# Decode attention with a gated feed-forward: keys transposed four sets ahead of their scores, the first four sets loaded between the gate's pieces

## The chip, the core and the metric

One core of a Trainium2 chip runs the whole program. The time is the device time of one execution in microseconds; of the kernel before there are three such runs. One further execution was recorded by the hardware profiler, and its trace is what the profile is made of.

## What is computed

Eight sequences, one new token each. The token is normalised, asks a window of 1024 cached keys per key-value head, and the attention's output is multiplied by a gate that a feed-forward network computes from the same normalised token:

```python
xn = _layernorm(x)                              # x: 8 x 1 x 512, bf16
q = (xn @ wq).reshape(B, 1, 32, 128)            # 32 query heads
k = k_cache[:, :, Sk - W:, :]                   # 8 x 8 heads, last W = 1024 of 4096 keys, 128 wide
v = v_cache[:, :, Sk - W:, :]                   # each key-value head serves 4 query heads
p = softmax((q . k) * 128 ** -0.5)
s = (p . v).reshape(B, 1, 4096) @ wo
g = silu((gelu(xn @ w_gate) * (xn @ w_up)) @ w_down)   # hidden width 1792
out = x + s * g
```

## The kernel before

A *group* is one pair of sequence and key-value head: 1024 keys by 128 numbers. There are 64 groups. A *set* is four groups (QG = NB = 4), so there are 16 sets (NQ), and one set of keys or of values is one load of 1 MB.

**Loads.** All large loads stand in the queue of SyncE (SP) in the order of lines 164 to 177: four pieces of the gate and up weights (`load_up`, 0.9 MB each), two of the down weights (`load_down`), four of Wq (`load_q`, 1 MB), the keys of sets 0 and 1, and then, for each set q, the keys of set q + 2, the values of set q, and after every second set 0.5 MB of Wo. They add up to 47.46 MB. All but Wo go through one ring of 16 buffers of 1 MB (`ring`, NRING, line 75): the seventeenth load waits until everything that reads the first has run.

**Front.** While the first weights come, TensorE runs constant products (`keep_busy`, line 233: a 128 x 128 matrix of ones by 512 columns of ones, into a PSUM tile that nobody reads). Then come the transposes of the normalised token, the products of the four pieces of gate and up (`ffn_up`, L274), GELU on VectorE and ScalarE (`ffn_act`, three steps, L288 to L307), the down products (`ffn_down`, L313), SiLU (`ffn_gate`), and the query products (L349), copied to `qT_all` (L358). After each of these pieces stands a `keep_busy`.

**Loop.** Lines 512 to 535 write out the order of the work by hand; each engine runs its own instructions in that order. In pass q, for each of the four groups i:

- `transposes` of the next group: eight 128 x 128 products of keys with the identity into one of two PSUM buffers (L368), then a copy of five eighths by VectorE (kTa, L375) and of three eighths by ScalarE (kTb, L377) into one of three buffers of `kT_pool`;
- `scores` (L397) of this group: transposed keys as weights, 16 columns of queries. A set's four groups share one PSUM bank; a mask product (L386) opens it;
- `values` (L476) of the set q - 2 (LAG = 2), with their `sums` (L451) before the first group;
- in group 1 `max_all` of the set before (L416 to L426), in group 2 `exponentials` of it: a second mask product (L437) adds the maximum, and ScalarE takes the exponential (L446).

At the end of a pass stand `normalise` of the finished set (L487) and `max_keys` (L408) of the set just scored. Two sets later the output projection of a key-value head (`project`, L502) is mixed in. After the last pass the last four heads are projected, multiplied by the gate, transposed, added to x and written out (lines 538 to 547).

The order of the front, in the kernel's own lines:

```python
    for n in range(NDC):
        ffn_up(n)
        keep_busy(5)
    for step in range(3):
        ffn_act(step)
    keep_busy(4)
    for d in range(NDC):
        ffn_down(d)
        keep_busy(2)
```

Of the kernel before, what the change touches and what calls it, by code (L numbers as in the profile page):

```python
# [11 lines left out]
BF16 = mybir.dt.bfloat16  # L12
# [5 lines left out]
def kernel(  # L18
# [33 lines left out]
    nc = tc.nc  # L52
# [3 lines left out]
    Hkv, Sk, Dh = A_k_cache.shape[1], A_k_cache.shape[2], A_k_cache.shape[3]  # L56
    Hq = A_wq.shape[1] // Dh
    rep = Hq // Hkv
    W = min(4096, max(256, Sk // 4))
    win0 = Sk - W  # L60
    F = B_w_gate.shape[1]
    P = nc.NUM_PARTITIONS
    NDC = D // P
    NFC = F // P
    NSC = W // P
# [5 lines left out]
    NB = QG  # L71
    NCS = QG * NSC
    VC = 4
    AC = 3
    NRING = 16
    MASK = -1.0e30
    NG = Hkv * B
    NQ = NG // QG
    QC = QG * rep
    SH = B // QG  # L80
    LAG = 2
# [3 lines left out]
    persist = ctx.enter_context(tc.tile_pool(name="persist", bufs=1))  # L85
    ffn_sb = ctx.enter_context(tc.tile_pool(name="ffn_sb", bufs=1))
    ring = ctx.enter_context(tc.tile_pool(name="ring", bufs=NRING))
    kT_pool = ctx.enter_context(tc.tile_pool(name="kT_pool", bufs=3))
    p_pool = ctx.enter_context(tc.tile_pool(name="p_pool", bufs=4))
    small = ctx.enter_context(tc.tile_pool(name="small", bufs=2))  # L90
    ps_misc = ctx.enter_context(tc.tile_pool(name="ps_misc", bufs=1, space=PSUM))
    ps_kT = ctx.enter_context(tc.tile_pool(name="ps_kT", bufs=2, space=PSUM))
# [16 lines left out]
    q_sb, up_sb, dn_sb, k_sb, v_sb = {}, {}, {}, {}, {}  # L109

    def buffer(n):
        return ring.tile([P, NL], BF16, name="ring_sb")[:, 0:n]

    def load_set(cache, q):
        hkv, b = divmod(q * QG, B)
        t = buffer(NL)
        nc.sync.dma_start(
            out=t,
            in_=cache[b : b + QG, hkv, win0:Sk, :].rearrange(
                "g (e c) d -> e g (c d)", c=NCS  # L120
            ),
        )
        return t

    def load_k(q):
        k_sb[q] = load_set(A_k_cache, q)

    def load_v(q):
        v_sb[q] = load_set(A_v_cache, q)

    def load_q(k):
        q_sb[k] = buffer(Hq * Dh)
        nc.sync.dma_start(out=q_sb[k], in_=A_wq.rearrange("(p k) n -> p k n", k=NDC)[:, k, :])

    def load_up(n):

        w = (B_w_gate, B_w_up)[n % 2]
        k = n // 2 * UPK
        up_sb[n] = buffer(UPK * F).rearrange("p (k n) -> p k n", k=UPK)
        nc.sync.dma_start(  # L140
            out=up_sb[n],
            in_=w.rearrange("(p k) n -> p k n", k=NDC)[:, k : k + UPK, :],
        )

    def load_down(n):
        dn_sb[n] = buffer(DNJ * D).rearrange("p (j d) -> p j d", j=DNJ)
        nc.sync.dma_start(
            out=dn_sb[n],
            in_=B_w_down.rearrange("(p j) d -> p j d", j=NFC)[
                :, n * DNJ : (n + 1) * DNJ, :  # L150
            ],
        )

    def load_wo(hkv):
        nc.sync.dma_start(
            out=wo_sb[:, hkv * rep : (hkv + 1) * rep, :],
            in_=A_wo[hkv * rep * Dh : (hkv + 1) * rep * Dh, :].rearrange(
                "(k p) d -> p k d", p=P
            ),
        )  # L160
# [2 lines left out]
    nc.scalar.dma_start(out=x_sb, in_=A_x.flatten_outer_dims())  # L163
    for n in range(NDC):
        load_up(n)
    for n in range(2):
        load_down(n)
    for k in range(NDC):
        load_q(k)
    for q in range(LAG):  # L170
        load_k(q)
    for q in range(NQ):
        if q + LAG < NQ:
            load_k(q + LAG)
        load_v(q)
        if q % SH == SH - 1:
            load_wo(q // SH)
# [4 lines left out]
    ident = consts.tile([P, P], BF16, name="ident")  # L182
    nc.vector.memset(ident, 0.0)
    nc.gpsimd.affine_select(
        out=ident,
        in_=ident,
# [14 lines left out]
        out=row_of,  # L201
        in_=row_of,
# [9 lines left out]
        out=other,  # L212
        in_=other,
# [19 lines left out]
    def keep_busy(n):  # L233
        for _ in range(n):
            nc.tensor.matmul(idle_ps, ones_w[:, 0:P], ones_w, start=True, stop=True)  # L235

    keep_busy(8)


    stats = persist.tile([B, nc.vector.BN_STATS_DIM], FP32, name="stats")  # L240
# [5 lines left out]
        out=rstd, in_=mv[:, 1:2], func=ACT.Sqrt, bias=eps_sb, scale=1.0  # L246
# [4 lines left out]
        out=xhat,  # L251
# [7 lines left out]
    for k in range(NDC):  # L259
        nc.tensor.transpose(  # L260
            xnT_ps[:, k, :], xhat[:, k::NDC], ident[0:B, 0:B]
        )
    nc.vector.tensor_copy(out=xnT_sb, in_=xnT_ps)


    ffn = {}

    def ffn_up(n):
        if n == 0:
            ffn["gu"] = ps_misc.tile([P, NFC, 2, B], FP32, name="gu_ps", tag="misc")  # L270
        for j in range(NFC):
            for i in range(UPK):
                k = n // 2 * UPK + i
                nc.tensor.matmul(  # L274
                    ffn["gu"][:, j, n % 2, :],
                    up_sb[n][:, i, j::NFC],
                    xnT_sb[:, k, :],
                    start=(n == 0 and j == 0 and i == 0),
                    stop=(k == NDC - 1),
                    skip_group_check=True,  # L280
                )

    def ffn_act(step):
        zT = ffn["gu"][:, :, 0, :]
        uT = ffn["gu"][:, :, 1, :]
        if step == 0:
            z2 = ffn["z2"] = ffn_sb.tile([P, NFC, B], FP32, name="z2")
            nc.scalar.activation(out=z2, in_=zT, func=ACT.Square)  # L288
        elif step == 1:
            z2 = ffn["z2"]  # L290
            nc.vector.tensor_scalar(  # L291
                out=z2, in0=z2, scalar1=0.044715, scalar2=1.0, op0=ALU.mult, op1=ALU.add
            )
            u3 = ffn_sb.tile([P, NFC, B], FP32, name="u3")
            nc.vector.tensor_tensor(out=u3, in0=z2, in1=zT, op=ALU.mult)
            th = ffn["th"] = ffn_sb.tile([P, NFC, B], FP32, name="th")
            nc.scalar.activation(
                out=th, in_=u3, func=ACT.Tanh, scale=0.7978845608028654
            )
        else:  # L300
            gm = ffn_sb.tile([P, NFC, B], FP32, name="gm")
            nc.vector.tensor_scalar(
                out=gm, in0=ffn["th"], scalar1=0.5, scalar2=0.5, op0=ALU.mult, op1=ALU.add
            )
            gz = ffn_sb.tile([P, NFC, B], FP32, name="gz")
            nc.vector.tensor_tensor(out=gz, in0=gm, in1=zT, op=ALU.mult)
            nc.vector.tensor_tensor(out=hT_sb, in0=gz, in1=uT, op=ALU.mult)  # L307
# [24 lines left out]

    for n in range(NDC):
        ffn_up(n)
        keep_busy(5)
    for step in range(3):
        ffn_act(step)
    keep_busy(4)
    for d in range(NDC):
        ffn_down(d)  # L340
        keep_busy(2)
    for step in range(2):
        ffn_gate(step)

# [2 lines left out]
    for k in range(NDC):  # L347
        for m in range(Hq):
            nc.tensor.matmul(  # L349
                qT_ps[:, m, :],  # L350
                q_sb[k][:, m * Dh : (m + 1) * Dh],
                xnT_sb[:, k, :],
                start=(k == 0 and m == 0),
                stop=(k == NDC - 1),
                skip_group_check=True,
            )
        keep_busy(5 if k < NDC - 1 else 3)
    nc.vector.tensor_copy(out=qT_all, in_=qT_ps.rearrange("p h b -> p b h"))  # L358


    kT, sc, pT, mxs, shift, recip = {}, {}, {}, {}, {}, {}

    def transposes(g):
        q, i = divmod(g, NB)
        kT_ps = ps_kT.tile([P, W], BF16, name="kT_ps")
        for c in range(NSC):
            n = i * NSC + c
            nc.tensor.transpose(  # L368
                kT_ps[:, c * P : (c + 1) * P],
                k_sb[q][:, n * Dh : (n + 1) * Dh],  # L370
                ident,
            )
        own = (NSC - AC) * P
        ta = kT_pool.tile([P, own], BF16, name="kTa")
        nc.vector.tensor_copy(out=ta, in_=kT_ps[:, 0:own])  # L375
        tb = kT_pool.tile([P, W - own], BF16, name="kTb")
        nc.scalar.copy(out=tb, in_=kT_ps[:, own:])  # L377
        kT[g] = [ta[:, c * P : (c + 1) * P] for c in range(NSC - AC)]
        kT[g] += [tb[:, c * P : (c + 1) * P] for c in range(AC)]

    def scores(g):
        q, i = divmod(g, NB)
# [126 lines left out]
            )  # L509


    transposes(0)
    for q in range(NQ + LAG):
        v = q - LAG
        for i in range(NB):
            g = q * NB + i
            if g + 1 < NG:
                transposes(g + 1)
            if i == 1 and 1 <= q <= NQ:
                max_all(q - 1)  # L520
            if g < NG:
                scores(g)
            if v >= 0:
                if i == 0:
                    sums(v)
                values(v * NB + i)
            if i == 2 and 1 <= q <= NQ:
                exponentials(q - 1)
            if v >= SH and v % SH == 0 and i >= NB // 2:
                for h in range(2):  # L530
                    project((v // SH - 1) * rep + (i - NB // 2) * 2 + h)
        if v >= 0:
            normalise(v)
        if q < NQ:
            max_keys(q)
# [42 lines left out]
```

## Time and profile before

| | us |
|---|---|
| median of three runs (lowest, highest) | 127.41 (127.36, 128.65) |
| the profiled execution | 127.63 |
| its span, first to last instruction | 125.8 |
| first gate piece landed, its first product | 5.82 |
| loop: first transposes | 33.45 |
| last load issued by SP | 104.79 |
| output's DMA issued | 123.42 |

The span is what the trace covers; the execution's time holds some 1.8 us around it. In the profile PE is TensorE, DVE VectorE, ACT ScalarE, SP SyncE; "L368" is line 368 of the kernel. A line of the chain of waits gives a start, a length, the engine, the tile written, the line and the number of instructions merged. The chain is followed back from the last instruction, at each step to what released it. A matmul's own duration holds its passage through the array, so durations of a run of matmuls overlap; how fast they go is read from the length of a run divided by their number. A line of the windows gives the busy time of PE, its weight load, DVE, ACT and POOL with the number of instructions, then the granted TensorE clock, the busy share of the DMA engines and GB/s.

### The profile page before, as it was taken

Reading aid. Unit: us, or ns where it says so; the run is one execution under the profiler, and the core shown is the slowest. Engines: PE = TensorE matmul, PEld = TensorE weight load, DVE = VectorE, ACT = ScalarE, POOL = GpSimd, SP = SyncE. Lnnn points to the kernel's source line nnn. Section 1 sums busy time; section 2 is a strip of 40 time slices with the busy share of each in tenths; the row PEclk is TensorE's granted clock in tenths of the full one; section 3 lists DMA queues with packets and bytes.
Section 4 is the critical chain, followed back from the end, with each engine's and each line's share of the span. In section 5 each row is a group of like instructions: output and inputs, shape, how many; then the busy total and the mean of one; then the engine's idle time right before and its main releaser. Section 6 shows DMA issues by size and latency. Waiting matters only on the chain.

```text
span 125.8 us, 4887 instructions
## 1 busy us (share of the span) xinstructions
PE 114.7 (91%) x2197; PEld 89.6 (71%) x2202; DVE 64.5 (51%) x200; ACT 42.5 (34%) x86; POOL 1.2 (1%) x7
## 2 busy tenths in 40 slices
PE   5899999989989999999999898989999999988780
PEld 1366663657777788887888787878787877877570
DVE  5200003010248768756786664858667677765531
ACT  4000005000054644543534254354544435352210
POOL 3000000000000000000000000000000000000000
PEclk9999999999999999999999999999999999999999
DMA  4999999999999999999999999999999999998300
GB/s 89 410 431 417 429 412 417 419 432 427 417 414 398 427 417 417 402 421 435 412 398 431 419 401 424 412 417 412 413 435 410 411 432 411 407 411 357 135 5 3
DMA packets 10325, 47.78 MB, mean 380 GB/s; under 512 B 816, under 2 KB 4928, under 8 KB 5696
## 3 DMA queue, kind: packets, MB, share of 16 engines
q1 hardware_dynamic: 10288, 47.46, 92.5%
q8 instruction: 17, 0.28, 0.9%
q14 instruction: 4, 0.03, 0.1%
q10 hardware_dynamic: 16, 0.01, 0.0%
HBM read 47.46 MB, written 0.01 MB: 377 GB/s over the span
## 4 chain that ended last, share of the span: by engine, by line
PE 73%; DVE 9%; ACT 6%; issue 5%; DMA 4%; ACTq 0%; DVEq 0%
PE kT_ps L368 19%; PE idle_ps L235 12%; PE o_ps L476 10%; PE sc_ps L397 9%; DVE kTa L375 6%; ACT kTb L377 6%; PE gu_ps L274 5%; DMA ring_sb<-in_B_w_gate_dram 4%; PE sc_ps L437 4%; PE sc_ps L386 4%; PE sT_ps L502 3%; PE sums_ps L451 3%; PE qT_ps L349 3%; PE fT_ps L313 1%; DVE mx L408 0%
## 5 line engine op out<-in xcount | busy, mean ns | idle before, releaser
L377 ACT COPY kTb<-kT_ps 128x384 bf16<-128x384 bf16 x64 | 30.6, 479 | 52.6 <-DVE kTa L375 52.6
L375 DVE COPY kTa<-kT_ps 128x640 bf16<-128x640 bf16 x64 | 31.3, 489 | 20.7 <-PE kT_ps L368 20.3
L368 PE MATMUL kT_ps<-ident,ring_sb 128*128 128x128 bf16 x512 | 39.1, 219 | 0.2 <-issue 0.2
L368 PEld LDWEIGHTS <-ring_sb 128*128 128x128 bf16 x512 | 29.4, 97 | 2.4 <-issue 2.2
L476 PE MATMUL o_ps<-pT,ring_sb 128*128 128x64 bf16 (+1 forms) x512 | 25.2, 190 | 2.2 <-issue 2.2
L235 PE MATMUL idle_ps<-ones_w 128*128 128x512 bf16 x53 | 20.0, 521 | 2.2 <-DVE ones_w L181 1.5
L476 PEld LDWEIGHTS <-ring_sb 128*128 128x128 bf16 x512 | 19.1, 97 | 3.0 <-issue 2.8
L397 PE MATMUL sc_ps<-qT_all,kTa 128*128 128x16 bf16 x320 | 17.8, 171 | 0.0
L397 PEld LDWEIGHTS <-kTa 128*128 128x128 bf16 x320 | 14.7, 96 | 4.2 <-issue 2.3
L397 PE MATMUL sc_ps<-qT_all,kTb 128*128 128x16 bf16 x192 | 14.5, 171 | 1.6 <-ACT kTb L377 0.4
L235 PEld LDWEIGHTS <-ones_w 128*128 128x128 bf16 x58 | 6.0, 121 | 8.8 <-issue 6.1
L397 PEld LDWEIGHTS <-kTb 128*128 128x128 bf16 x192 | 9.3, 96 | 3.3 <-ACT kTb L377 1.0
L408 DVE TENSOR_REDUCE mx<-sc_ps 128x16 f32<-128x512 f32 x16 | 10.9, 681 | 0.0
L446 ACT ACTIVATE pT<-sc_ps 128x512 bf16<-128x512 f32 x16 | 9.6, 601 | 2.7 <-PE sc_ps L437 2.6
L274 PEld LDWEIGHTS <-ring_sb 128*128 128x128 bf16 x112 | 7.4, 162 | 2.2 <-issue 1.6
L274 PE MATMUL gu_ps<-xnT_sb,ring_sb 128*128 128x8 bf16 x112 | 7.3, 201 | 0.5 <-DMA ring_sb<-in_B_w_gate_dram 0.5
L291 DVE TENSOR_SCALAR z<-z 128x112 f32<-128x112 f32 x1 | 0.2, 219 | 13.7 <-ACT z L288 13.7
L437 PE MATMUL sc_ps<-diag,ones_pp 48*128 48x512 bf16 x16 | 6.2, 386 | 0.4 <-DVE diag L426 0.4
L451 PE MATMUL sums_ps<-pT,ones_pp 128*128 128x64 bf16 x128 | 6.3, 192 | 0.0
L386 PE MATMUL sc_ps<-other,row_of 4*128 4x512 bf16 x16 | 6.2, 385 | 0.0
L502 PEld LDWEIGHTS <-wo_sb 128*128 128x128 bf16 x128 | 4.3, 96 | 2.5 <-issue 2.5
L502 PE MATMUL sT_ps<-oT_all,wo_sb 128*128 128x8 bf16 x128 | 5.4, 167 | 0.3 <-DVE oT_all L487 0.3
(54 smaller groups left out, 59.4 us busy)
## 6 DMA issues: line engine op xcount, KB each, us to landing
ring_sb<-in_A_k_cache_dram SPq DMA_DIRECT2D x16, 1024.0 KB, 18.8
ring_sb<-in_A_v_cache_dram SPq DMA_DIRECT2D x16, 1024.0 KB, 18.6
ring_sb<-in_A_wq_dram SPq DMA_DIRECT2D x4, 1024.0 KB, 19.5
wo_sb<-in_A_wo_dram SPq DMA_DIRECT2D x8, 512.0 KB, 17.8
ring_sb<-in_B_w_gate_dram SPq DMA_DIRECT2D x2, 896.0 KB, 5.0
ring_sb<-in_B_w_up_dram SPq DMA_DIRECT2D x2, 896.0 KB, 8.4
ring_sb<-in_B_w_down_dram SPq DMA_DIRECT2D x2, 896.0 KB, 12.9
x_sb<-in_A_x_dram ACTq DMA_DIRECT2D x1, 8.0 KB
```

Source lines behind the costliest of these rows:

```text
L235: nc.tensor.matmul(idle_ps, ones_w[:, 0:P], ones_w, start=True, stop=True)
L274: nc.tensor.matmul(ffn["gu"][:, j, n % 2, :], up_sb[n][:, i, j::NFC], xnT_sb[:, k, :], start=(n == 0 and j == 0 and i == 0), stop=(k == ND ...
L368: nc.tensor.transpose(kT_ps[:, c * P : (c + 1) * P], k_sb[q][:, n * Dh : (n + 1) * Dh], ident,)
L375: nc.vector.tensor_copy(out=ta, in_=kT_ps[:, 0:own])
L377: nc.scalar.copy(out=tb, in_=kT_ps[:, own:])
L386: nc.tensor.matmul(sc[q], row_of.rearrange("g e s -> g (e s)"), other.rearrange("g s j -> g (s j)") .unsqueeze(1) .to_broadcast([QG, NCS, ...
L397: nc.tensor.matmul(sc[q][:, i * NSC + c, :], kT[g][c], qT_all[:, b : b + QG, hkv * rep : (hkv + 1) * rep], start=False, stop=False, skip_g ...
L408: nc.vector.tensor_reduce(out=mx, in_=sc[q].rearrange("p c n -> p n c"), axis=AX.X, op=ALU.max)
L437: nc.tensor.matmul(sc[q], ones_pp[0 : LO + QC, :], shift[q].unsqueeze(1).to_broadcast([LO + QC, NCS, QC]), start=False, stop=True, skip_gr ...
L451: nc.tensor.matmul(sums_ps, ones_pp, pT[q][:, c * NB : (c + 1) * NB, :], start=(c == 0), stop=(c == NSC - 1),)
L476: nc.tensor.matmul(o_ps[q][:, 0:wide, :], v_sb[q][:, n * Dh : (n + 1) * Dh], pT[q][:, n : n + wide, :], start=(n == 0), stop=(n == NCS - 1 ...
L502: nc.tensor.matmul(sT_ps[0][:, d, :], wo_sb[:, h, d * P : (d + 1) * P], oT_all[:, h, :], start=(h == 0 and d == 0), stop=(h == Hq - 1), sk ...
```

## The change

The transposes run four sets ahead of the scores (LEAD = 4) instead of one group. The keys of the first four sets are loaded alternately with the four gate pieces, and each set is transposed after the piece before it; all `keep_busy` after the first, which has six products instead of eight, are taken out. Further keys are loaded four sets earlier than before, counted against the values. `kT_pool` grows from 3 to 19 buffers, the ring shrinks from 16 to 12. The GELU steps stand before the transposes of set 3. `transposes` itself is unchanged and only moves up in the file.

```diff
-    NRING = 16
+    NRING = 12
+    LEAD = 4
-    kT_pool = ctx.enter_context(tc.tile_pool(name="kT_pool", bufs=3))
+    kT_pool = ctx.enter_context(tc.tile_pool(name="kT_pool", bufs=LEAD * NB + 3))
     for n in range(NDC):
         load_up(n)
+        load_k(n)
...
-    for q in range(LAG):
+    for q in range(LEAD, LEAD + LAG):
         load_k(q)
     for q in range(NQ):
-        if q + LAG < NQ:
-            load_k(q + LAG)
+        if q + LEAD + LAG < NQ:
+            load_k(q + LEAD + LAG)
         load_v(q)
...
-    keep_busy(8)
+    keep_busy(6)
...
     for n in range(NDC):
         ffn_up(n)
-        keep_busy(5)
-    for step in range(3):
-        ffn_act(step)
-    keep_busy(4)
+        if n == NDC - 1:
+            for step in range(3):
+                ffn_act(step)
+        for i in range(NB):
+            transposes(n * NB + i)
     for d in range(NDC):
         ffn_down(d)
-        keep_busy(2)
...
-        keep_busy(5 if k < NDC - 1 else 3)
...
-    transposes(0)
     for q in range(NQ + LAG):
         v = q - LAG
         for i in range(NB):
             g = q * NB + i
-            if g + 1 < NG:
-                transposes(g + 1)
+            if g + LEAD * NB < NG:
+                transposes(g + LEAD * NB)
```

## The prediction

> **What bounds it now.** I read the page first (busy shares, slices, chain shares), then the chain of waits in order of time, then the windows of the last microseconds.
>
> ```profile
> span 125.8 us, 4887 instructions
> PE 114.7 (91%) x2197; PEld 89.6 (71%) x2202; DVE 64.5 (51%) x200; ACT 42.5 (34%) x86; POOL 1.2 (1%) x7
> PE 73%; DVE 9%; ACT 6%; issue 5%; DMA 4%; ACTq 0%; DVEq 0%
> q1 hardware_dynamic: 10288, 47.46, 92.5%
> ```
>
> Two resources are nearly full: TensorE (91%) and the 16 DMA engines (92.5%). The chain is TensorE's, with data waited for only at its head (4%). The chain in order of time shows how fast TensorE goes:
>
> ```profile
> 15.20 2.15 PE idle_ps L235 x5
> 17.35 1.61 PE gu_ps L274 x28
> 19.20 3.62 PE idle_ps L235 x8
> 22.82 0.35 PE fT_ps L313 x14
> ...
> 29.18 1.10 PE idle_ps L235 x5
> 30.28 0.78 PE qT_ps L349 x32
> ...
> 33.61 0.46 PE kT_ps L368 x8
> 34.09 0.50 DVE kTa L375
> 34.62 0.49 ACT kTb L377
> 35.38 0.48 PE kT_ps L368 x8
> ...
> 42.56 0.32 PE sc_ps L386
> ...
> 111.92 0.32 PE sc_ps L386
> ...
> 120.51 0.92 PE o_ps L476 x32
> ```
>
> A 512-column product takes 0.43 us up to 22.6 us (2.15/5) and 0.22 afterwards (1.10/5); a narrow one 57 ns (1.61/28), then 25 (0.35/14). So TensorE ran at half rate for 22.6 us, although the granted-clock column says 1.00 there. What raised it stands before the switch: eight constant products back to back, 19.20 to 22.6. The same eight from 1.52 on (to 4.93 at 0.43 each) did not, nor did 13 us of 2.15 us constant products alternating with 1.61 us of narrow ones.
>
> The mask product L386 opens each set: from 42.56 to 111.92 are 13 sets, 5.33 us each. Adding the parts of a set (transposes 4 x 0.46, scores 4 x 0.29, values 4 x 0.25, sums 0.25, two masks 0.64, maximum 0.11, projection 0.29) gives 5.28: TensorE is packed, and its waits for the two copies (DVE 9% and ACT 6% of the chain) lie beside scores and values and cost it some 0.05 us a set. The values end at 121.43; 4.4 us of projection, output and its DMA end the span.
>
> ```profile
> 115.00:116.00 1.00, 0.95 (x21) 0.65 (x18) 0.88 (x3) 0.29 (x1) 0.00 (x0) 1.00 0.81 318
> 118.00:119.00 1.00, 0.64 (x17) 0.60 (x16) 0.93 (x4) 0.00 (x0) 0.00 (x0) 1.00 0.30 105
> 119.00:120.00 1.00, 0.94 (x25) 0.64 (x25) 0.03 (x2) 0.53 (x1) 0.00 (x0) 1.00 0.00 0
> 125.60:125.70 0.10, 0.00 (x0) 0.00 (x0) 0.00 (x0) 0.00 (x0) 0.00 (x0) 0.50 0.00 0
> ```
>
> The last two columns are DMA share and GB/s, before them the clock. The input stream ends at 119.0, only 2.4 us ahead of the last values. The last line is the clock falling to half after the last product (122.96): the 3.4 us before it hold four 128-column and a few 8-column products, some 0.2 us of columns, 6%.
>
> **The profiled run** took 127.63, 1.83 more than its span; the median of the three runs is 127.41. I sum against 127.63 and take off 0.2.
>
> **The change, part by part.**
>
> *The stream.* Bytes are the same, so its end stays at 119.0. At the page's 417 GB/s, anchored on the first piece (0.92 MB, landed at 5.8), a load lands at 3.6 us + MB/0.417. In the new order: K set 0 (1.97 MB) 8.3; the gate's pieces 1 to 3 at 10.5, 15.2, 20.0 with K 1 to 3 between and after, K 3 at 22.5; down 26.9; last piece of Wq (13.9 MB) 36.9, where the old order (9.7 MB) gave 26.9; K 4 39.4; V 0 (18.1 MB) 47.0 instead of about 37; then one V every 5.67 us (2.36 MB a set) to V 9 at 97.3; V 15 between 116.1 and 117.7.
>
> *Ring of 12 instead of 16.* A load waits for the readers of the load 12 earlier. V 1 waits for set 3's transposes (at the latest 31 by the sum below) and the stream reaches it at 49.5; K 15 waits for K 9's transposes in pass 5 (about 75) and is reached at 92. SP's queue holds these waits, and behind them only further loads stand, with 18 us in hand. Cost nothing; if TensorE were 18 us later, the stream would wait too.
>
> *Constant products.* 52 go: 24 after the gate pieces at 0.43 = 10.2 us of TensorE, 26 in the down and query products at 0.22 = 5.6, and 2 at the start, in front of x-hat. None carries data. Their time is filled by transposes or by waits for data; their other effect, the clock, is priced below.
>
> *Sixteen transpose groups moved to the front.* Passes 12 to 15 lose 16 x 0.46 = 7.4 us of TensorE, 1.84 each. Their 32 copies move too: at the front DVE and ACT are idle but for the GELU steps, which stand in their queues before the copies of set 3. That chain took 2.7 us (19.0 to 21.7); two groups fill the two PSUM buffers, the other two wait for it, and so do the down products behind them.
>
> *Copies no longer waited for by scores*: 0.05 x 12 passes, 0.6 us at most, by the packing above. I put nothing.
>
> *Front at half rate.* A transpose is 128 columns, so a quarter of 0.43: 0.107 us, 0.85 a group. With two buffers a group takes (0.85 + 0.49 + 0.48 + about 0.25 of hand-overs)/2 = 1.04; a set 4.15 (at full rate 1.77 for two groups, 3.55). Gate piece 0 runs 5.8 to 7.5, set 0 8.3 to 12.4, then 1.65 + 4.15 alternately: piece 3 ends at 25.4, GELU at 28.2, set 3 at 31.0; down 56 x 57 ns = 3.2, 34.2; gate 0.8, 35.0; four query blocks of 1.84, 42.3. At full rate the pieces wait for data instead (3.55 + 0.8 is under the 4.73 us of a pair's bytes), queries end at about 38, and pass 0 starts when K 4 lands, 39.4. In the old kernel it started at 34.4.
>
> *Which rate?* Transposes at half rate cover 0.85 of 1.04 us with columns, 82%. The trace has a stretch of 62 to 65% that did not raise the clock (2.15 us of constant products per 3.77) and one of 100% that did; 82% lies midway. The down and query products cover 4% of their time (32 x 8 columns per 2.5 us of bytes), for 8 us: next to the 6% after which the clock fell. So pass 0 starts at half rate almost surely; whether the front did I put at two to one for half rate, since the eight products of 1.52 to 4.93 also failed.
>
> The Trainium skill, "TensorE: Matmul & The Clock Gate", Part 4, speaks against the change: by it, transposes don't count as busy and full rate doesn't engage for them. No row of the old kernel can show it, for there transposes always ran among other products. Taken at its word, the clock would stay down and the sum would be that of the third rival. Part 1 there would have one busy window of some 3.4 us suffice, which the first eight products here contradict.
>
> *Pass 0 and on.* Half-rate pass 0: mask 0.43 + 4 x (0.85 + 8 x 57 ns) = 5.7 us against 3.84 in the old trace (34.44 to 38.28), columns 73 to 80%. A half-rate later pass is 3.41 + 3.68 + 0.46 + 0.86 + 0.2 + 0.46 = 9.1, so 3.7 more. For the time until the clock is back the bounds are one eight-product stretch (3.4 us) and never; I take the first pass, by the 3.4 us row.
>
> *Sum.* Pass 0 from 42.3 to 48.0; pass 1 4.2 (old 38.28 to 42.49), 52.2; passes 2 to 11 10 x 5.33, 105.5; passes 12 to 15 at 3.6, 119.9 (5.33 - 1.84 = 3.49 is the packing; the step from maximum through masks to the exponential, which transposes covered, may add up to 0.3); pass 16 2.8 and pass 17 1.3 as in the old trace, 124.0. That is 2.6 later than 121.43: 130.2 for the profiled run, 130.0 by the median.
>
> **The rivals.**
> 1. *Faster: the clock is up from the front on and holds through the query products.* Pass 0 at 39.4, pass 2 at 47.4, pass 11 at 96.0 with V 9 landing just then, 101.4; 4 x 3.6, 2.8 and 1.3: 119.9, so 1.5 less, 125.9. If passes 12 to 15 kept up with the stream (3.15 us for 1.31 MB), the values would end 0.9 after V 15, 118.9: 124.9, the floor. It decides if the products at 31 to 39 us run at 25 ns. For it: transposes are half of a set's columns in the old loop, and the clock held there. Against: the 6% row.
> 2. *Front up, pass 0 down*: 39.4 + 5.7 + 4.2 + 53.3 + 14.4 + 4.1 = 121.1, 0.3 less: 127.1, no difference.
> 3. *Slower by much: the loop doesn't raise the clock soon.* Each further half-rate pass adds 3.7: two more give 137; all of them 42.3 + 5.7 + 6.6 + 10 x 9.1 + 4 x 5.7 + 5.8 = 174, a time of about 180. For it: 73 to 80% lies below the 100% that was needed. Against: masks and sums lift some 3.4 us stretches to 88%.
> 4. *The change doesn't free the loop*: with V ten us later in the stream, TensorE waits for values in the middle passes. At full rate pass 11 may start at 96.0 by data and at 95.4 by work, so this costs 0.6, and is in rival 1.
>
> **How the numbers follow.** About 1% (126.1 to 128.7) is what can be told from no change. Rival 1 gets 0.25, rival 2 0.15, the forecast and its neighbours (a front or one more pass at half rate, 128.7 to 134) 0.38, rival 3 beyond 134 0.22. The range runs from the floor, 125.0, to two further half-rate passes, 137; what is left out is some 0.04 below and 0.14 above. The forecast's own range is 128 to 133.
>
> **What would show it.** Right: the query products at 57 ns; set 3's transposes ending near 31; pass 0's first mask at 42 to 43; sets at 5.3 us afterwards; the stream ending at 119 as before; the clock column at 0.50 somewhere from 31 to 48. Wrong: products of 25 ns before 20 us or at 31 to 39, a first mask before 40.5 (rival 1 or 2); transposes at 0.85 a group beyond 55 us (rival 3); gaps in the stream before 115 (the ring). Passes 12 to 15 at more than 3.9 us would upset the end of every sum.

## The result and the profile after

The changed kernel takes 131.56 us (median of four, 131.28 to 131.64) against 127.38 in the runs beside it: a ratio of 1.0347, 95% interval 1.0293 to 1.04. It is slower by 3.5%; the forecast was 130.0, range 125 to 137. The ratios and their intervals leave out runs more than 1.5% above the fastest of their kernel; the medians hold all runs.

The page of the changed kernel (span, busy times, granted clock in 40 slices of 3.24 us, chain by engine, the input queue):

```profile
span 129.6 us, 4764 instructions
PE 107.6 (83%) x2150; PEld 92.2 (71%) x2150; DVE 65.0 (50%) x200; ACT 42.7 (33%) x86; POOL 1.2 (1%) x7
PEclk9977856855555599999999999869999999996555
PE 45%; DMA 42%; issue 4%; DVE 3%; SPq 3%; ACT 1%; ACTq 0%
q1 hardware_dynamic: 10288, 47.46, 89.7%
```

TensorE is less busy (83%, not 91%), and data now makes 42% of the chain, not 4%. In the kernel before the clock column read:

```profile
PEclk9999999999999999999999999999999999999999
```

The column counts as full rate all that lies before the trace's first clock event, which stands at 23.16 us there and at 4.68 here. In the changed kernel it shows the clock going up and down in the front, lying at half from 25 to 45.6 us, dipping at 83, and staying at half from 117 on. The chain in order of time (L390 is the mask that opens a set, L386 before):

```profile
20.58 19.61 DMA ring_sb<-in_A_k_cache_dram
40.23 1.04 PE kT_ps L275 x8
41.27 0.54 PE sc_ps L390
...
45.99 0.32 PE sc_ps L390
...
50.04 0.32 PE sc_ps L390
...
75.25 18.81 DMA ring_sb<-in_A_v_cache_dram
94.10 0.41 PE o_ps L480 x8
...
103.11 0.37 PE sc_ps L390
...
114.32 0.32 PE sc_ps L390
...
116.39 1.57 issue
117.96 0.59 PE sc_ps L441
...
123.31 1.63 PE o_ps L480 x32
```

The loop opens when set 4's keys land. TensorE waits for values twice (0.63 us at 82.5, 0.37 at 94.1). The last values take 1.63 us where they took 0.92. The first mask of a pass, taken from both traces, shows where the time went. Two lines of the kernel before that the table needs, the first mask of pass 0 from its timeline and that of pass 12 from its chain:

```profile
34.44 0.38 PE L386 MATMUL sc_ps<-other,row_of 4*128 4x512 bf16 x1
```

```profile
95.82 0.32 PE sc_ps L386
```

| stretch | before, us | after, us | difference |
|---|---|---|---|
| start to first mask of pass 0 | 34.4 | 41.2 | +6.8 |
| passes 0 and 1 | 8.1 | 8.8 | +0.7 |
| passes 2 to 11 | 53.3 | 53.1 | -0.2 |
| passes 12 to 14 | 16.1 | 11.2 | -4.9 |
| pass 15 to the last values | 9.5 | 10.6 | +1.1 |
| last values to the end | 4.4 | 4.6 | +0.2 |

Taking the transposes out of the last passes does shorten passes 12 to 14, but by less than was lost at the start, and the stretch from pass 15 on, which lost three groups (1.4 us), got longer all the same.

### The profile page after: what moved, and what is told of

It is laid out like the page before. It is cut to its first block, busy times and chain, and to the rows that moved or that the text cites. A ratio compares the mean times of both kernels' runs of the same rounds, so it can differ in the third digit from the quotient of the medians.

```text
span 129.6 us, 4764 instructions
## 1 busy us (share of the span) xinstructions
PE 107.6 (83%) x2150; PEld 92.2 (71%) x2150; DVE 65.0 (50%) x200; ACT 42.7 (33%) x86; POOL 1.2 (1%) x7
## 4 chain that ended last, share of the span: by engine, by line
PE 45%; DMA 42%; issue 4%; DVE 3%; SPq 3%; ACT 1%; ACTq 0%
DMA ring_sb<-in_A_k_cache_dram 15%; DMA ring_sb<-in_A_v_cache_dram 15%; PE kT_ps L275 14%; DMA ring_sb<-in_B_w_up_dram 12%; PE o_ps L480 10%; PE sc_ps L401 7%; PE sc_ps L441 4%; PE sc_ps L390 3%; PE sT_ps L506 3%; PE sums_ps L455 3%; ACT pT L450 1%; SPq L118 1%; SPq L141 1%; DVE kTa L282 1%; PE mxT_ps L420 1%
## 5 line engine op out<-in xcount | busy, mean ns | idle before, releaser
L275 PE MATMUL kT_ps<-ident,ring_sb 128*128 128x128 bf16 x512 | 45.1, 243 | 7.0 <-ACT kTb L284 3.9
L275 PEld LDWEIGHTS <-ring_sb 128*128 128x128 bf16 x512 | 35.6, 110 | 9.3 <-issue 6.8
L480 PE MATMUL o_ps<-pT,ring_sb 128*128 128x64 bf16 (+1 forms) x512 | 26.5, 198 | 2.4 <-issue 1.4
L480 PEld LDWEIGHTS <-ring_sb 128*128 128x128 bf16 x512 | 20.8, 102 | 2.9 <-issue 1.6
L491 DVE TENSOR_TENSOR oT_all<-o_ps,recip 128x16 bf16<-128x16 f32 x16 | 3.6, 228 | 9.6 <-PE o_ps L480 9.6
L441 PE MATMUL sc_ps<-diag,ones_pp 48*128 48x512 bf16 x16 | 6.7, 421 | 2.0 <-issue 1.6
L297 PEld LDWEIGHTS <-ring_sb 128*128 128x128 bf16 x112 | 7.2, 158 | 0.2
L372 PE MATMUL qT_ps<-xnT_sb,ring_sb 128*128 128x8 bf16 x128 | 4.0, 168 | 3.7 <-DMA ring_sb<-in_A_wq_dram 2.9
L390 PE MATMUL sc_ps<-other,row_of 4*128 4x512 bf16 x16 | 6.3, 396 | 0.4 <-ACT pT L450 0.4
L372 PEld LDWEIGHTS <-ring_sb 128*128 128x128 bf16 x128 | 3.8, 104 | 4.0 <-DMA ring_sb<-in_A_wq_dram 3.1
## 6 DMA issues: line engine op xcount, KB each, us to landing
ring_sb<-in_B_w_up_dram SPq DMA_DIRECT2D x2, 896.0 KB, 16.1
```

Of the source, the lines that this page charges most:

```text
L275: nc.tensor.transpose(kT_ps[:, c * P : (c + 1) * P], k_sb[q][:, n * Dh : (n + 1) * Dh], ident,)
L297: nc.tensor.matmul(ffn["gu"][:, j, n % 2, :], up_sb[n][:, i, j::NFC], xnT_sb[:, k, :], start=(n == 0 and j == 0 and i == 0), stop=(k == ND ...
L390: nc.tensor.matmul(sc[q], row_of.rearrange("g e s -> g (e s)"), other.rearrange("g s j -> g (s j)") .unsqueeze(1) .to_broadcast([QG, NCS, ...
L441: nc.tensor.matmul(sc[q], ones_pp[0 : LO + QC, :], shift[q].unsqueeze(1).to_broadcast([LO + QC, NCS, QC]), start=False, stop=True, skip_gr ...
L480: nc.tensor.matmul(o_ps[q][:, 0:wide, :], v_sb[q][:, n * Dh : (n + 1) * Dh], pT[q][:, n : n + wide, :], start=(n == 0), stop=(n == NCS - 1 ...
```

## Experiments

No kernel leaves any of the computation out; they differ in constant products, which carry no data, in the order of the work and in buffers. Three theories stood at first on where the loss comes from. Theory 1: the clock, which lies at half rate at the end. Theory 2: the late and half-rate start of the loop, carried to the end. Theory 3: the order of the stream, which puts Wq and the values 10 us later. Theories 2 and 3 don't exclude each other.

**Constant products put back.** Into the changed kernel: at the end (from pass 15), in the front, and both. The cores of the edits, with remarks added:

```diff
+            keep_up(q, i)          # 16 products in passes 15 to 17
             if v >= 0:
                 if i == 0:
                     sums(v)
```

```diff
             transposes(n * NB + i)
+            if n == NDC - 1 and i == 1:
+                keep_busy(8)
     for d in range(NDC):
         ffn_down(d)
+        keep_busy(2)
...
+        keep_busy(6)               # after each query block
```

> The changed kernel with 16 constant products (128x512, no data) spread over passes 15 to 17, in PSUM that the transposes have left. Theory 1, the loss is the clock at the end: from 117.3 us on the changed kernel ran at half rate, and masks, sums, values and projections there sum to 2.5 us more than at full rate; with the clock held the time falls by 2 to 2.5, to 129.0 to 129.6. Theory 2, the loss is the late, half-rate start of the loop (40.2 instead of 34.4, pass 0 5.1 instead of 3.8), carried to the end: the time stays at 131.6 or rises by up to 1.5 for the products. Theory 3, the values arrive ten us later in the stream and TensorE ends late whatever its rate: no gain either, 131 to 132.

Ratio 1.0359 (1.026 to 1.0458), median 133.86: no gain. In its trace, which is of the longest of its four runs (131.18 to 135.0), the clock had fallen at 108.8, in pass 13, before the first product, and rose again only at 122.5; the products themselves ran at half rate until then. So this run doesn't test theory 1; the later run with products from pass 12 on does.

> The changed kernel with constant products in the front alone: 8 while GELU holds up set 3's copies, 2 after each down column, 6 after each query block, so that pass 0 runs at full rate. Theory 1 (the clock at the end): pass 0 shortens by 1.2, but TensorE waits for values at 82.5 and 94.1 us anyway, so the time stays within 0.6 of 131.6. Theory 2 (the start is carried to the end): 129.8 to 130.4. Theory 3 (order of the stream): no change.

Ratio 1.0382 (1.0328 to 1.0435), median 132.59: no gain, so the half rate of pass 0 is not what the end pays for. The products did what they were for: pass 2 opened at 48.7 instead of 50.0. The head start is lost to data. From its timeline, the instructions that waited for a load (idle time before them in brackets):

```profile
70.22 0.41 PE L484 MATMUL o_ps<-pT,ring_sb 128*128 128x64 bf16 x8 [0.93 <-DMA ring_sb<-in_A_v_cache_dram]
80.50 0.62 PE L275 MATMUL kT_ps<-ident,ring_sb 128*128 128x128 bf16 x8 [1.62 <-DMA ring_sb<-in_A_k_cache_dram]
82.97 0.61 PE L484 MATMUL o_ps<-pT,ring_sb 128*128 128x64 bf16 x8 [0.79 <-DMA ring_sb<-in_A_v_cache_dram]
```

Three waits, 3.3 us against 1.0 in the changed kernel. The clock also fell for 6.8 us at 81.4, after the second of them, and pass 12 opens at 103.7, 0.6 later than without the products. Here TensorE came earlier to these passes and waited for the stream.

> Both sets of constant products. Theory 1: as with those at the end alone, 129.0 to 129.6. Theory 2: as with those of the front alone, or worse by the cost of the others, 130 to 131.5. Theory 3: 131 to 132.

Ratio 1.0224 (1.0162 to 1.0285), median 131.98. The ratio rests on two of the four runs, 130.08 and 130.62. They lie in theory 2's range, and the interval lies below the changed kernel's (1.0293 to 1.04): a gain of about a point, though measured beside other runs, that neither set gave clearly alone and theory 3 didn't forecast. The trace is of a run of 133.34 (pass 12 again at 103.2, the clock down from 109.6 to 119.9) and can't show where the gain comes from; that stays open.

> The changed kernel with constant products from pass 12 on: three in each of passes 12 to 15 (two of them where TensorE waits for DVE or ACT anyway), one more in pass 15, five in pass 16, two in pass 17. Theory 1, now sharper: in passes without transposes the products cover only 37 to 39% of a 3.41 us stretch (columns at the granted rate, counted by the rows they use), and in all traces so far the clock fell after stretches of 36% and less and held at 37% and more; products that started at pass 15 came too late, since there the clock had fallen in pass 13. With three products a pass the cover is 50 to 57%, the clock holds to the end in most executions, values end near 122.8 instead of 124.95 and the time is 129 to 130 against 131.6. Theory 3 (the order of the stream alone): no gain, the 19 products cost up to 2 us, 132 to 133.5.

Three products in each of passes 12 to 15 and eight more, 20 in all (the expectation says 19). Ratio 1.0242 (1.0157 to 1.0327), median 131.11: between theory 1's 129 to 130 and theory 3's 132 to 133.5. The interval overlaps that of the changed kernel, so a gain isn't shown. The clock held to the end in the profiled run:

```profile
123.85 0.92 PE o_ps L480 x32
```

The last values took 0.92 us, not 1.63. Yet they end at 124.77 instead of 124.94. The trace has two waits without a releaser there, 0.90 and 0.58 us, and records of 14 of the 20 products, so part of those waits may be products. So theory 1's mechanism is seen, some 2.5 us of half-rate work by the durations after 117.3, but these constant products and the waits took about as much as the clock gave.

**A shorter lead.** LEAD = 2 with a ring of 14, and LEAD = 1 with a ring of 15:

```diff
-    NRING = 12
-    LEAD = 4
+    NRING = 14
+    LEAD = 2
...
     for n in range(NDC):
         load_up(n)
-        load_k(n)
+        if n < LEAD:
+            load_k(n)
...
-        for i in range(NB):
-            transposes(n * NB + i)
+        if n < LEAD:
+            for i in range(NB):
+                transposes(n * NB + i)
```

> The changed kernel with a lead of two sets instead of four (two sets of keys between the gate's pieces, ring of 14), so the query weights and all values come 2.1 MB, 5 us, earlier, and passes 12 and 13 keep their transposes. Theory 3: pass 0 starts near 35, TensorE no longer waits for values, and the time falls by 2 to 4, to 127.5 to 129.5. Theory 1: the end still drops to half rate unless the transposes cover it; 129 to 131.6. Theory 2: 5 us earlier start, 128 to 129.

> The changed kernel with a lead of one set (one set of keys after the first gate piece, ring of 15). Theory 3: each set of lead puts Wq and the values 2.5 us later in the stream; with 131.6 for four sets and 130.1 for two, one set gives 128 to 129. If only four sets were too many: 130; if the lead itself pays: below 126.7.

Ratios 1.0188 (1.012 to 1.0256) and 1.0025 (0.9978 to 1.0072), medians 130.14 and 127.66. Less lead, less time, which is theory 3's direction; but the first lies above its range and in theory 1's (the clock fell at 118.6), and the second 0.3 below its range. Pass 0 opens at 36.0 and 34.1, pass 12 at 98.5 and 96.3. TensorE did not stop waiting for loads, as theory 3 had it: in the loop 2.0 us with two sets and 2.5 with one, 1.0 with four. (The trace with two sets is of the shortest of its runs, 128.78.)

> Lead of two sets as before, with the constant products of passes 14 to 17 alone. Theory 1: its clock fell at 118.6 and cost some 1.5 us; held, the time falls from 130.1 (fast runs 128.8 on) to 127.5 to 128.5. If the clock's fall there cost nothing: 130 to 131.

> The same and constant products after the pieces and query blocks, so that pass 0 runs at full rate (it saves 1.2 us there). Theory 1: TensorE waits for values later, so no more than 0.5 from the run without them. Theory 2 (the start is carried to the end): 1 to 1.5 us less than the run without them.

Ratios 1.0088 (1.0047 to 1.013) and 1.0068 (1.0022 to 1.0114), medians 129.62 and 129.19. That is about a point less than LEAD = 2 alone, with intervals that just touch; 129.62 lies between the two ranges of its expectation. Between the two, theory 2 asked for 1 to 1.5 us; the ratios differ by 0.2 points and the medians by 0.4, but the intervals overlap and don't settle it.

**The parts of the change alone, on the kernel before.** First without the later constant products; then, each time on top of that, with the changed order of loads (the loads' part of the change's diff), with a ring of 12, and with products at the end. The first edit:

```diff
     for n in range(NDC):
         ffn_up(n)
-        keep_busy(5)
...
-    keep_busy(4)
...
-        keep_busy(2)
...
-        keep_busy(5 if k < NDC - 1 else 3)
```

> The kernel before with all constant products after the first eight taken out, order of loads and transposes as before: that part of the change alone. By the cover theory the loop's transposes at half rate cover over 74% within one to three stretches and raise the clock, and they last to pass 14 and hold it; the loop starts near 29 instead of 34.4 and loses 2 to 4 us at half rate: 125.5 to 127.5. If constant products were what keeps the kernel at full rate, or transposes did not count for the clock: 135 and more, up to 180.

Ratio 0.9854 (0.9775 to 0.9933), median 126.72, within its forecast of 125.5 to 127.5. The products were not needed: the clock rose at 36.0, 4.1 us after the first mask. Its chain where the loop opens, and at its last values:

```profile
9.91 20.09 DMA ring_sb<-in_A_k_cache_dram
30.00 0.05 issue
30.05 1.89 PE kT_ps L364 x16
31.93 0.54 PE sc_ps L382
...
119.11 1.63 PE o_ps L472 x32
```

> The kernel before without the later constant products, and with the changed kernel's order of loads alone (four sets of keys between the gate's pieces, ring of 16); transposes stay one group ahead. Theory 3 (the order of the stream sets the pace): queries can't end before the last piece of Wq at 37, pass 0 begins near 39 instead of 31.9, pass 12 near 101 to 103, its last passes keep their transposes, and the time is 131 to 135. If the order of loads costs nothing and the emptied last passes or the clock are the whole loss: 126 to 128.

The chain of this one at the same places:

```profile
17.67 20.51 DMA ring_sb<-in_A_wq_dram
38.23 1.02 PE qT_ps L348 x32
39.24 1.73 PE kT_ps L366 x16
...
127.58 0.92 PE o_ps L474 x32
```

Ratio 1.0607 (1.0519 to 1.0695), median 135.37, 0.4 above theory 3's range. Transposes are where they were; the order of the loads alone moves the first mask from 31.9 to 40.9 and the end of the last values from 120.7 to 128.5, although the clock, once up at 44.9, held at full rate to the end. Nearly all of the delay at the start arrives at the end. TensorE's waits for loads in the loop don't make it: they sum to 1.3 us here and to 1.7 without the changed order.

> The kernel before without the later constant products, with a ring of 12 buffers instead of 16: the other part of the change that stands alone. If buffers come free 18 us ahead of the stream, as the prediction says: no difference from 16 buffers, within 0.6 of 126.7. If the ring holds up the stream: gaps in it, 128 and more.

Ratio 0.9963 (0.9913 to 1.0013), median 126.70 against 126.72 with 16 buffers. By the ratios, taken beside different runs of the kernel before, it is 1.1 points more, with intervals that overlap: no loss that can be told, though one of a point isn't excluded.

> The kernel before without the later constant products, and with ten of them in passes 15 to 17, most where TensorE waits for the maximum. In the profiled run of the version without them the clock fell at 117.9 and the last values took 1.63 us instead of 0.92; in one whose clock held the span was 1.0 less. Theory 1: the clock holds, 126.0 to 126.5 (from 126.7). If the products cost what they save: 126.7 to 127.5.

Ratio 1.0036 (0.9992 to 1.0081), median 127.57: the clock holds until 124.6, after the last values, and the products cost more than it gives.

**What follows.** Put in steps: without constant products and with 12 buffers 0.9963; with the order of loads 1.0607 (ring of 16, measured beside it); with the transposes moved to the front as well, which is the changed kernel, 1.0347 (measured earlier, beside other runs). So the order of loads costs 6.4 points, some 8 us; the moved transposes give about 2.6 points, some 3.3 us, back; dropping the products gives 0.4 to 1.5 points. The order of loads is the cause (theory 3), and it acts through the start of the loop: the first mask comes 8.4 to 9 us later, and that delay is carried to the end, as theory 2 has it, but with no part for the half rate of pass 0. The query weights were not moved apart from the values, so it stays open how much an earlier opening would gain before TensorE waits for the values. The clock at the end (theory 1) comes on top; how much of the changed kernel's time it costs isn't settled. Of all versions only the one without constant products and otherwise as before has an interval under the kernel before: 0.7 to 2.3% in one comparison and, with 12 buffers, from 0.9% to none in another.

## Why the prediction was right, and where it was not

The side and the size were right, and so was the outline: the front is late, the end pays. But the front is late for another reason than the prediction put first, and that the sum came out is in part luck. With pass 0 beginning at 40.2 and lasting 5.1 us, as measured, the prediction's own sum is 40.2 + 5.1 + 4.2 + 53.3 + 14.4 + 4.1 = 121.3 for the last values, where the kernel before had 121.4: no difference. A cost that was too high in the front made up for one that was too low at the end. Step by step:

- *The stream*'s last load landed at 119.1, in the kernel before at 119.4 (forecast: no change), and the stream had no gap; *the ring* cost nothing that its run can tell.
- *Where pass 0 starts* was mis-sized: 40.2 by the landing of K 4 (forecast of that landing 39.4), not 42.3 by TensorE, which had the queries done at 38.5. The step that failed is "a narrow one 57 ns, then 25", read as a sign of the clock. Two lines of the changed kernel's windows, one over gate piece 1 and one over a query block (the clock is the third figure from the end):

```profile
11.60:13.20 1.60, 1.60 (x31) 1.60 (x29) 0.55 (x2) 0.96 (x2) 0.00 (x0) 1.00 1.01 422
34.00:36.00 2.00, 0.98 (x32) 0.93 (x32) 0.00 (x0) 0.00 (x0) 0.00 (x0) 0.50 1.04 434
```

  The 28 gate products fill 1.6 us at full clock; they start 60 ns apart, just as they do at half clock in the kernel before. The 32 query products take some 0.9 us at half clock (0.98 with the last one's passage); they start 27 ns apart, against 25 at full clock in the kernel before. So the difference of 57 and 25 goes with the operand, not with the clock. The gate product's weights are read with a stride (`j::NFC`), the query's are not, and on the page of the changed kernel their weight loads take 158 and 104 ns in the mean; that the stride is the reason is argued from this, no run changes it alone. The prediction's own lines held the answer: the first 14 down products (22.82, 0.35 us) ran at 25 ns before the trace's first clock event at 23.16. Wider products do slow down: those of the values, 64 columns, start 29 ns apart at full clock and 53 at half. So down, queries and scores cost at half rate nearly what they cost at full, and pass 0 took 5.1 us from its first transposes, not 5.7.
- *The signs it named.* Query products at 57 ns and a first mask at 42 to 43 didn't come: they ran at 27 ns, which the prediction had taken as a sign that the clock is up, and the mask came at 41.2. Set 3's transposes ended at 29.4 (forecast 31). The sets of 5.3 us, the end of the stream and the half clock between 31 and 48 came.
- *Which rate in the front*: it was neither. The clock rose at 4.7, 11.5 and 21.8 and fell 3.4 us later each time; where the queries run it was down, as forecast, and it came back at 45.6, after pass 0's last scores, also as forecast (there at 48.0).
- *Passes 2 to 11*: 53.1, forecast 53.3. *Passes 12 to 14*: 11.2, forecast 10.8.
- *Pass 15 to the last values*: forecast 7.7 at full rate, measured 10.6. This is the term that was too small, by 2.9. Passes 12 to 15 lose 15 groups of transposes, not 16 (pass 15 held three), but that doesn't enter the sum. A wait of 1.57 us without a releaser stands at 116.4, and the clock fell at 117.3; how it divides between the two isn't shown. The errors add up: 2.4 early at pass 12, 0.4 late in passes 12 to 14 and 2.9 late after them, which left the sum 0.9 short at the last values.
- *Rival 3's "all passes at half rate"* is excluded, and with it the Trainium skill's Part 4 of "TensorE: Matmul & The Clock Gate" as it would bear here: from 8.1 to 11.5 TensorE ran nothing but transposes, and the clock rose at 11.5. (They are written as `nc.tensor.transpose`; the trace lists them as MATMUL.) *Rival 4*, the order of the stream, was the cause, but not on the path that it named: waits for values in the middle passes, priced at 0.6 us, took 1.0. The order acted through the opening of the loop, which the prediction had in its paragraph on the stream, but hid behind TensorE's 42.3.

How the clock is decided can now be read. The clock's events in a trace lie on a grid of 3.413 us: all times between two of them are multiples of it. For each stretch of the grid I added up the columns of all matmuls at the granted rate, each weighted by the share of the array's rows and columns it uses (a mask product with 48 rows counts 48/128), and divided by 3.413:

| kernel, stretch | cover | clock after it |
|---|---|---|
| before, 2.7 to 6.1 (the first eight constant products lie across two stretches) | 66% | stays at half |
| before, 19.7 to 23.2 | 90% | rises |
| changed, 1.3 to 4.7 (six constant products inside one stretch) | 75% | rises |
| changed, 8.1 to 11.5 (transposes) | 87% | rises |
| changed, 11.5 to 14.9 | 32% | falls |
| changed, 42.2 to 45.6 | 91% | rises |
| changed, 79.8 to 83.2 (wait for values) | 36% | falls |
| changed, 107.1 to 110.5 | 39% | stays at full |
| changed, 110.5 to 113.9 | 37% | stays at full |
| changed, 113.9 to 117.3 (wait of 1.57) | 31% | falls |
| before, 115.3 to 118.7 | 40% | stays at full |

In the fourteen traces of this study no stretch of 37% and more lost full rate, and all of 36% and less did, but one of 32% in which its run's work ended (changed order of loads, 126.8 to 130.3). From half rate all of 77% and more rose; up to 73% only two (68 and 69%) did; from 74 to 76% both happened. The lower limit was fitted to the first traces, written into an expectation, and held in the later ones but for that one stretch; the upper one is not as sharp, as one later trace shows alone (products from pass 12 on: down after 75%, up after 68%). This also answers the prediction's remark that the first eight constant products contradict a single busy window of 3.4 us: they filled neither of their two stretches (35 and 66%). Taking the transposes out of the last four passes leaves them at 37 to 39%, just above the lower limit; the stretch with the wait of 1.57 us fell below it.

## What to carry to other kernels

A load that is moved forward in a full queue moves everything behind it back by its own bytes: price it at the consumer that opens the loop (here 4.2 MB, 10 us, before the query weights), not at the work it lets you hide. Work taken off a busy engine late and put into an idle stretch early did pay here, some 3.3 us, but less than the 8 us that its early data cost by delaying what starts the loop. Before a duration is read as a sign of the clock, compare the same instruction at both rates.

## What was unexpected

Besides the grid and the cover, TensorE stops for 0.2 to 1.6 us with nothing in the profile that it waits for. In the changed kernel such waits end at 68.4, 74.6, 80.8, 105.8, 111.8 and 118.0, each 2.3 to 2.6 us after a 16 KB packet of the instruction queue begins (the first at 65.9, the last at 115.5); in the kernel before the longest lay at 112.9 to 113.5, after a packet at 111.2. All fourteen traces agree: each of the 62 such waits of 0.18 us and more after 45 us ends 2.2 to 2.6 us after such a packet begins, though many packets have no wait behind them. That these are waits for instructions is argued from the times alone. What sets their length isn't shown: the longest, 1.57 us, lies in a pass without transposes, but so does one of 0.19. That the longest is what let the clock fall at 117.3 fits its stretch's cover of 31% against 37 to 39% in the three before; no run removes it alone.
